# A fused attention and GEGLU kernel on one core: the scale chain split around the scores, one product split, a copy and an eviction exchanged

## The chip, the core and the metric

The kernel runs on one core of one Trainium2 chip. The metric is the device time of one execution in microseconds (us); below, times come from three runs and from one profiled execution. Engines are named as in the profile: PE (TensorE matmul), PEld (its weight loads), DVE (VectorE), ACT (ScalarE), POOL (GpSimd), SP (SyncE, which issues the DMAs).

## What is computed

Two branches of the same x (2048 x 576, float32) are mixed by a gate. Branch a is attention with 32 heads of width 18, in four segments of 512 rows, each with a causal softmax and a compressive memory of the earlier segments. Branch b is a feed-forward layer of width 4608.

```python
x = A_x                                            # 1 x 2048 x 576
g = sigmoid((x * gate_w).sum(-1, keepdims=True))
# a, per head and segment s:
logits = qs @ ks.T * 18**-0.5 + causal_mask
a_dot  = softmax(logits) @ vs
a_mem  = (phi(qs) @ M) / (phi(qs) @ z + 1e-6)      # M, z summed over earlier segments
o      = sigmoid(beta) * a_mem + (1 - sigmoid(beta)) * a_dot
a      = concat(o) @ wo
# b:
b = (gelu(x @ w_gate) * (x @ w_up)) @ w_down
out = g * a + (1 - g) * b
```

## The kernel before

Float32 numbers go through PE as pairs of 16-bit words (a high word and a low word, each product as three matmuls), and some products are formed from sums of blocks, as in Strassen's scheme, so that fewer matmuls are needed. Powers of two scale each pair; they are found from sums of squares of the weights.

After the projections the kernel runs 72 steps, `step(v)` for v = 0 to 71. A step does one 128-column block f = v // 2 of the feed-forward's width for one half p = v % 2 of the rows. Four steps share two blocks f, called a round here: fb = v // 4, i4 = v % 4. Steps 4 to 67 carry one attention head each (k = v - 4; `on(k)` says so) besides the feed-forward work. In step v stand:

- The products of the hidden layer, into three PSUM banks: V, X (the bank "G") and Y (the bank "U"). `product` adds six matmuls, for two 128-row blocks k and three pairs of words each. X gets A11 at the step's start; `dve.tensor_copy(Y, X)` then copies it into Y, and PE goes on adding to both: S2 and S1 to Y, A12 to X. Y's contents are taken to SBUF (`gl` or `hold`) by DVE several times, after which PE adds the next product.
- `down`: the second feed-forward matmul of the round before, in chains of six matmuls of 288 columns into the two banks "dn"; DVE evicts each chain into `acc` (L1283). Three chains (`early`) stand before the scores and five (the rest of `early`, and `late`) behind them.
- `scores`: eight matmuls of the two units 2k and 2k + 1 of a head, into two banks "dn", two "st" and a half each of "pv". A put, `put(a, i)`, is DVE's eviction of one of them with the mask added and the maximum taken (L1189). Unit 2k is put in the same step; of unit 2k + 1 the pieces 1 and 0 are put at the step's end and 3 and 2 (bank "st") in the next step, as `put(2 * k - 1, ...)`.
- `powers` (ACT and POOL): exponentials, a high word on ACT (L1208), a low word by subtraction on POOL (L1209), then a transposing DMA. `values` (PE) and `normalize` (DVE) follow a step later.
- The weights of the next round: `scale_g`, `scale_d` (DVE, L307 and L394), high words on ACT (L341), low words on POOL (L345), sums on POOL.
- Once in a round, in the step i4 = 1, `scales(fb + 1)` computes the powers of two for the next round from a matmul of the sums of squares with ones (L94): a reduction, a multiply with maximum and four bit operations on DVE, all on 2 or 4 columns. `scales_out` makes the scales themselves on POOL (L281 to L289).

Every engine works through its instructions in the order in which the code issues them (`manual_schedule` over PE, ACT, DVE and POOL); only the DMA queue of SP is ordered by the scheduler. So the place of a line in `step` is its place in the engine's queue.

At the end `out_step` does the product with `wo`, in banks of 288 columns that DVE adds into `acc` (L1778), and `store` sends rows out. The last product of all is done in two halves of 144 columns, each with its own eviction and store.

Of the kernel before, what the change touches and what calls it, by code (L numbers as in the profile page):

```python
# [8 lines left out]
F32 = mybir.dt.float32  # L9
BF16 = mybir.dt.bfloat16  # L10
F16 = mybir.dt.float16
I32 = mybir.dt.int32
# [6 lines left out]
P = 128  # L19
# [24 lines left out]
def kernel(ctx: ExitStack, tc: tile.TileContext, xs, wqk, wv, wo, wgu, wd, beta, out):  # L44
# [216 lines left out]

    scl_a = {}

    def scales(fb, o=None):

        o = sums(stat[fb % 2].rearrange("p a b -> p (a b)"), o)
        z = wts.tile([P, 6], F32, name="z", tag="z", bufs=2)
        dve.tensor_reduce(z[:, 4:6], o.rearrange("p (a b) -> p a b", a=2), AX.X, OP.add)
        dve.tensor_scalar(z[:, 0:4], x2, z[:, 4:5], 1e-30, OP.mult, OP.max)  # L269
        v = wts.tile([P, 2, 2], F32, name="v", tag="v", bufs=2)  # L270
        pb = wts.tile([P, 2, 4], F32, name="pb", tag="pb", bufs=3)
        dve.tensor_scalar(v[:, 0].bitcast(I32), z[:, 4:6].bitcast(I32), 1, EXP, OP.logical_shift_right, OP.bitwise_and)
        dve.tensor_scalar(pb[:, 0].bitcast(I32), z[:, 0:4].bitcast(I32), EXP, None, OP.bitwise_and)
        dve.tensor_scalar(v[:, 1].bitcast(I32), v[:, 0].bitcast(I32), EXP, None, OP.bitwise_xor)
        dve.tensor_scalar(pb[:, 1].bitcast(I32), pb[:, 0].bitcast(I32), EXP, None, OP.bitwise_xor)
        scl_a[fb] = v, pb

    def scales_out(fb):
        v, pb = scl_a.pop(fb)
        sc = wts.tile([P, 10], F32, name="sc", tag="sc", bufs=3)  # L280
        pool.tensor_scalar(sc[:, 0:2], v[:, 1], 2.0**-51, None, OP.mult)  # L281
        pool.tensor_scalar(sc[:, 2:6], xis, v[:, 0, 0:1], 2.0**50, OP.mult, OP.mult)
        pool.tensor_scalar(sc[:, 6:10], pb[:, 1], 2.0**14, None, OP.mult)
        pool.tensor_tensor(sc[:, 6:10], sc[:, 6:10], sc[:, 2:6], OP.mult)
        if fb:
            w = wts.tile([P, 4], F32, name="we", tag="we", bufs=2)
            pool.tensor_scalar(w, scl[fb - 1][1][:, 0], v[:, 0, 1:2], 2.0**35, OP.mult, OP.mult)
            ev = wts.tile([P, 16], F32, name="ev", tag="ev", bufs=2)
            pool.tensor_tensor(ev.rearrange("p (c q) -> p c q", c=4),  # L289
                               gate[:, 1].rearrange("p (c q) -> p c q", c=4),  # L290
                               w.unsqueeze(2).to_broadcast([P, 4, 4]), OP.mult)
            evs[fb - 1] = ev
        scl[fb] = (sc, pb)
# [229 lines left out]
    def gl_tile():  # L523
        return mp2.tile([P, L], F32, name="gl", bufs=3)

    def product(o, f, a, x, h, l, start=False):

        w = pair_g[f]
        for k in range(2):
            for i, b in ((0, h), (0, l), (1, h)):  # L530
                pe.matmul(o, w[:, i, (a + k) * P : (a + k + 1) * P], x[:, b + k],  # L531
                          start=start and k == 0 and i == 0 and b == h, stop=k == 1 and i == 1,
                          skip_group_check=True)
# [581 lines left out]
    with tc.tile_pool(name="keep", bufs=2, side="right", reuse_waits="tile") as kp, ExitStack() as tail:  # L1115
# [332 lines left out]
        def step(v):  # L1448
# [33 lines left out]
            if v == 4:  # L1482
                dve.tensor_copy(Y, X)
                nest((1, 0), 2)
                some(0, early[:2])
                nest((1, 0), 3)
                wait = []
                down(0, early[2] // 2, early[2] % 2, wait)
                nest_last(fb, V, p)
                dve.tensor_copy(g1, V)  # L1490
                wait.pop()()
                nest_pairs_x(1, 1)
                some(0, early[3:4])
            elif fb and i4 < 2:
                nest_last(fb, V, p)
                dve.tensor_copy(g1, V)
                dve.tensor_copy(Y, X)
                put(2 * k - 1, 3)
            else:
                put(2 * k - 1, 3)  # L1500
                dve.tensor_copy(Y, X)  # L1501
            if v == 0:
                last_sum(1, 1)
            if v == 1:
# [63 lines left out]
                scales_out(fb + 1)  # L1568
            if both and i4 != 1:
                normalize(k - 2)  # L1570
            product(X, f, A12, x1, 2, 6)
            if v != 3 and not on(k):
                rest(X, f, U4, x1, (0,) if fb else (0, 1))
            if fb > 1 and i4 == 1:
                scales(fb + 1, bank("pv") if on(k) else None)
            some(fb - 1, early[max(one, 2):3])
            if v == 5:
                scales(fb + 1, bank("pv") if on(k) else None)
            product(Y, f, S1, t, 0, 2)
            rest(Y, f, G4, x2_, (0,) if fb else (0, 1))  # L1580
            if v == 3:
                rest(X, f, U4, x1)
            if on(k):
                scores(k, (f, V, G4, x1, 0), (f, X, U4, x1, 0), (f, Y, G4, x2_, 64))
                rest(X, f, U4, x1, (0,))
            elif fb:
                low_rests(f, (V, G4, x1), (Y, G4, x2_))
# [13 lines left out]
                put(2 * k, i)  # L1601
            if low is not None and on(k):
                result_low(low)
            rear = list(early[3 + (v == 4) :])
            if not on(k):
                some(fb - 1, rear)
# [18 lines left out]
            if on(k):  # L1625
                some(fb - 1, rear[:-1])
                nest(at, 0)
                some(fb - 1, rear[-1:])
                nest(at, 1)
                put(2 * k + 1, 1)  # L1630
                puts.pop(2 * k)
                weights_nest(fb, i4, "late")
                powers(2 * k)
                some(fb - 1, late[:1])
                ends.append((f, c, X, g0))
                end_first()
                some(fb - 1, late[1:2])
                nest(at, 2)
                some(fb - 1, late[2:])
                if on(k - 1):  # L1640
                    values(2 * k - 2)
                nest(at, 3)
            else:
                if v != 3:
                    nest(at, 0)
                some(fb - 1, late[:1])
                if v != 3:
                    nest(at, 1)
                weights_nest(fb, i4, "late")
                some(fb - 1, late[1:])  # L1650
                if v != 3:
                    nest(at, 2)
                if on(k - 1):
                    values(2 * k - 2)
                if fb:
                    low_rests(f, (X, U4, x1), (Y, UG, x2_))
                    ends.append((f, c, X, g0))
                    if at or i4 == 1:
                        end_first()
                if v != 3:  # L1660
                    nest(at, 3)
            ends.append((f, e, Y, g1))
# [122 lines left out]
        def out_step(u, p):  # L1785

            x, y = 2 * u, 2 * u + 1
            S = lambda n: lambda i, k: sums_o[u][:, i, 2 * (0, 3, 0, 2, 1)[n] + k]
            A = lambda t, k0: lambda i, k: ot[t][:, 4 * i + k0 + k]
            if p == 7:  # L1790
                V = ob3[u, "V"] = bank("pv" if u % 2 else "V")
                out_product(V, S(3), T3, True)
                out_rest(V, y, R2)
                put_out(V, y, 1)
            if p == 1:
                X, Y = bank("U" if u % 2 else "G"), bank("st", 2)
                ob3[u, "X"], ob3[u, "Y"] = X, Y
                out_product(X, A(x, 0), B11, True)
                dve.tensor_copy(Y[:, :NH], X[:, :NH])
            if p == 4:  # L1800
                V = ob3[u, "V"]
                out_product(V, A(y, 2), T4)
                out_rest(V, y, RD)
                put_out(V, y, 0)
            if p == 2:
                X = ob3[u, "X"]
                out_product(X, A(x, 2), B21)
                out_rest(X, x, R1)
                put_out(X, x, 0)
            if p in (6, 5, 3):  # L1810
                Y = ob3[u, "Y"]
                if (u, p) == (NT - 1, 3):
                    for c in (slice(0, NH // 2), slice(NH // 2, NH)):
                        out_product(Y, S(4), B22, c=c)
                        out_rest(Y, x, R2, c)
                        put_out(Y, x, 1, c)
                        store(x, slice(NH + c.start, NH + c.stop))
                    return
                out_product(Y, S({6: 2, 5: 1, 3: 4}[p]), {6: T2, 5: T1, 3: B22}[p])
                if p == 3:  # L1820
                    out_rest(Y, x, R2)
                put_out(Y, *{6: (y, 0), 5: (y, 1), 3: (x, 1)}[p])
# [6 lines left out]
        with tc.manual_schedule(engines=ORDERED):  # L1829
# [40 lines left out]
            for u in range(NT):  # L1870
# [6 lines left out]
                for i, p in steps:  # L1877
                    out_step(u + i, p)
                    if u == NT - 1:
                        if p == 5:  # L1880
                            store(2 * u + 1, slice(NH, D))
                        if p == 4:
                            store(2 * u + 1, WHOLE)
                if u == NT - 2:
                    store(2 * u + 2, WHOLE)
                if u + 1 < NT:
# [48 lines left out]
```

## Time and profile before

| | before |
|---|---|
| three runs | 1577.87, 1579.21, 1580.11 us; median 1579.21 |
| profiled execution | 1574.72 us, of which the span from first to last instruction 1573.0 |
| granted TensorE clock | 0.999 |
| steps of a usual round (from score to score) | 17.8, 16.9, 19.2 and 19.2 us |
| ACT busy, POOL busy | 77%, 71% of the span |

In a row of the timeline the first number is the start in us from the span's start, the second the duration from the first to the last of the merged instructions; then engine, line and operation, `out<-in`, the shapes, a count, and in brackets how long the engine stood idle before it and what ended that. In a row of the waits stand the waiting engine, tile and line, what it waited for, and then total us, times and the longest. Rows of busy matmuls overlap by some 0.15 us, since their ends are modelled.

### The profile page before, as it was taken

Reading aid. Unit: us, or ns where it says so; the run is one execution under the profiler, and the core shown is the slowest. Engines: PE = TensorE matmul, PEld = TensorE weight load, DVE = VectorE, ACT = ScalarE, POOL = GpSimd, SP = SyncE. Lnnn points to the kernel's source line nnn. Section 1 sums busy time; section 2 is a strip of 40 time slices with the busy share of each in tenths; the row PEclk is TensorE's granted clock in tenths of the full one; section 3 lists DMA queues with packets and bytes.
Section 4 is the critical chain, followed back from the end, with each engine's and each line's share of the span. In section 5 each row is a group of like instructions: output and inputs, shape, how many; then the busy total and the mean of one; then the engine's idle time right before and its main releaser. Section 6 shows DMA issues by size and latency. Waiting matters only on the chain.

```text
span 1573.0 us, 33451 instructions
## 1 busy us (share of the span) xinstructions
PE 1549.2 (98%) x12204; PEld 965.4 (61%) x12204; DVE 1289.8 (82%) x3258; ACT 1213.5 (77%) x2059; POOL 1119.0 (71%) x1217
## 2 busy tenths in 40 slices
PE   9999999999999999999999999999999999999998
PEld 5765655565666656665656565666656566656577
DVE  7878976888888888888898888888888888787675
ACT  7667545888888888988888888888888988887421
POOL 4355566777777868686777777776868687777596
PEclk9999999999999999999999999999999999999999
DMA  6644441464657565566556574756566665555645
GB/s 242 235 151 150 150 130 41 105 138 109 136 118 153 115 136 121 127 133 121 132 113 134 107 153 105 145 114 161 116 139 127 126 138 122 128 104 102 126 86 167
DMA packets 483622, 206.69 MB, mean 131 GB/s; under 512 B 427264, under 2 KB 462464, under 8 KB 482944
## 3 DMA queue, kind: packets, MB, share of 16 engines
q1 hardware_dynamic: 483456, 204.56, 57.1%
q8 instruction: 95, 1.56, 0.4%
q14 instruction: 71, 0.58, 0.1%
HBM read 83.91 MB, written 31.98 MB: 74 GB/s over the span
## 4 chain that ended last, share of the span: by engine, by line
PE 86%; DVE 8%; ACT 2%; POOL 1%; issue 1%; DMA 1%; SPq 0%; POOLq 0%; DVEq 0%; ACTq 0%
PE dn L1273 23%; PE U L531 16%; PE G L531 11%; PE V L531 5%; PE V L1398 5%; PE pv L1226 4%; PE st L412 3%; PE U L1321 2%; PE dn L419 2%; DVE z L269 2%; PE G L412 1%; PE U L412 1%; PE G L1321 1%; PE st L1769 1%; PE U L1325 1%
## 5 line engine op out<-in xcount | busy, mean ns | idle before, releaser
L531 PEld LDWEIGHTS <-pairg 128*128 128x128 f16 x2592 | 247.8, 97 | 259.4 <-issue 10.1
L1273 PE MATMUL dn<-paird,hhr 128*128 128x288 f16 x2115 | 329.9, 286 | 0.1
L1207 ACT ACTIVATE pb<-pb,mb,esc 128x512 f32<-128x512 f32 (+3 forms) x512 | 304.9, 642 | 5.3
L1283 DVE SCALAR_TENSOR_TENSOR acc<-dn,ev,acc 128x288 f32<-128x288 f32 x533 | 267.3, 512 | 48.3 <-PE dn L1273 46.4
L1209 POOL TENSOR_TENSOR pl<-pb,ph 128x896 f16<-128x896 f32 (+1 forms) x128 | 182.0, 1442 | 161.0 <-ACT ph L1208 161.0
L1209 POOL TENSOR_TENSOR pb<-pb,ph 128x896 f16<-128x896 f32 (+1 forms) x128 | 179.5, 1402 | 107.5 <-ACT ph L1208 67.3
L1273 PEld LDWEIGHTS <-hhr 128*128 128x128 f16 x2160 | 210.2, 98 | 74.2 <-issue 1.0
L531 PE MATMUL U<-xt,pairg 128*128 128x512 f16 x864 | 209.9, 379 | 3.5 <-DVE U L1501 3.5
L531 PE MATMUL G<-x,pairg 128*128 128x512 f16 x864 | 209.9, 379 | 0.5 <-DVE gl L1298 0.5
L1273 PE MATMUL dn<-paird,hhd 128*128 128x288 f16 x1275 | 208.6, 286 | 0.0
L1208 ACT ACTIVATE ph<-pb 128x896 f16<-128x896 f32 (+1 forms) x256 | 188.6, 737 | 9.7
L345 POOL TENSOR_TENSOR pairg<-raw,pairg 128x384 f16<-128x384 f32 (+2 forms) x144 | 165.3, 1168 | 17.2 <-ACT pairg L341 17.2
L1273 PEld LDWEIGHTS <-hhd 128*128 128x128 f16 x1296 | 125.6, 98 | 47.4 <-issue 0.5
L1316 ACT ACTIVATE gl<-gl,sc 128x512 f32<-128x512 f32 x110 | 78.6, 717 | 42.2 <-DVE gl L1590 20.9
L1398 PE MATMUL V<-xt,nest 128*128 128x256 f16 x714 | 105.5, 272 | 1.0 <-DVE hold L1422 0.4
L531 PE MATMUL U<-x,pairg 128*128 128x512 f16 x432 | 104.9, 379 | 0.8 <-DVE gl L1590 0.8
L531 PE MATMUL V<-x,pairg 128*128 128x512 f16 x426 | 103.3, 378 | 0.1
L1189 DVE CUSTOM_DVE_ANT_0 pb<-st,mask 128x128 f32<-128x128 f32 (+2 forms) x192 | 96.6, 503 | 0.0
L1189 DVE CUSTOM_DVE_ANT_0 pb<-dn,mask 128x512 f32<-128x512 f32 (+2 forms) x192 | 91.9, 503 | 0.0
L1226 PEld LDWEIGHTS <-pt 128*128 128x128 f16 x2560 | 83.4, 96 | 6.3
L1313 POOL TENSOR_TENSOR hhr<-gl,hhr 128x512 f16<-128x512 f32 x64 | 78.6, 1234 | 11.2 <-ACT hhr L1305 11.2
L412 PEld LDWEIGHTS <-wp 128*128 128x128 f16 x504 | 48.7, 98 | 59.0 <-DVE wp L115 0.9
(367 smaller groups left out, 3244.7 us busy)
## 6 DMA issues: line engine op xcount, KB each, us to landing
raw<-in_wgu_dram SPq DMA_DIRECT2D x36, 640.0 KB
qkt<-qk SPq DMA_DIRECT2D x192, 108.0 KB
rawd<-in_wd_dram SPq DMA_DIRECT2D x36, 288.0 KB
qk<-stage SPq DMA_DIRECT2D x32, 256.0 KB
qk<-stage SPq DMA_DIRECT2D x40, 128.0 KB
vp<-vstage SPq DMA_DIRECT2D x16, 296.0 KB
vt<-vp SPq DMA_DIRECT2D x16, 296.0 KB
orow<-oa SPq DMA_DIRECT2D x16, 288.0 KB
```

Of the source, the lines that this page charges most:

```text
L345: pool.tensor_tensor(spot(f, *p, 1), raw_g[f][:, p[0] : p[1]], spot(f, *p, 0), OP.subtract)
L412: pe.matmul(o, w(k, a), x[:, i], start=n == 0, stop=n == 13, skip_group_check=True)
L531: pe.matmul(o, w[:, i, (a + k) * P : (a + k + 1) * P], x[:, b + k], start=start and k == 0 and i == 0 and b == h, stop=k == 1 and i == 1, ...
L1189: dve.tensor_tensor_reduce(scored(u, qi), out[u, qi], mask[:, L - (qi + 1) * P :], 1.0, -3e38, OP.add, OP.max, mx[u][:, qi : qi + 1])
L1207: act.activation(r, r, AF.Exp, bias=b[:, qi : qi + 1], scale=esc[:, 0, c : c + 1])
L1208: act.activation(h[:, cols], p, AF.Copy)
L1209: pool.tensor_tensor(low[:, cols], p, h[:, cols], OP.subtract)
L1226: pe.matmul(ov, pr[:, 10 * i + COL[qi] // P + kb], v[:, 4 * e + kb, c0 : c0 + VC], start=kb == 0 and i == 0, stop=kb == qi and i == 1)
L1273: pe.matmul(o[:, :NH], hh[:, a, q * P : (q + 1) * P], w[:, b, n * NH : (n + 1) * NH], start=i == 0, stop=i == 5)
L1283: dve.scalar_tensor_tensor(av, o[:, :NH], ev, av, OP.mult, OP.add)
L1313: pool.tensor_tensor(hh[:, 1], t, hh[:, 0], OP.subtract)
L1398: pe.matmul(o, w[:, (7 * c + i) * P : (7 * c + i + 1) * P], x[d], start=start and n == 0, stop=n == 2, skip_group_check=True)
```

## The change

The scale chain of a step i4 = 1 is split. The reduction stays; the multiply with maximum is issued on POOL, behind the score evictions in the text of the step; the bit operations follow there on DVE, with two of them merged into one over six columns. Half of the product A12 for X (its block k = 1) is issued behind the scores in steps that have scores. In steps with i4 of 2 or 3 (and in the first round) the copy of X to Y stands ahead of the put of piece 3 instead of behind it. In the one step behind the last head, the values come two lines later. The last output product is no longer halved.

```diff
--- before.py
+++ after.py
@@ -261,30 +261,37 @@
 
     scl_a = {}
 
-    def scales(fb, o=None):
+    def scales(fb, o=None, later=False):
 
         o = sums(stat[fb % 2].rearrange("p a b -> p (a b)"), o)
         z = wts.tile([P, 6], F32, name="z", tag="z", bufs=2)
         dve.tensor_reduce(z[:, 4:6], o.rearrange("p (a b) -> p a b", a=2), AX.X, OP.add)
-        dve.tensor_scalar(z[:, 0:4], x2, z[:, 4:5], 1e-30, OP.mult, OP.max)
-        v = wts.tile([P, 2, 2], F32, name="v", tag="v", bufs=2)
-        pb = wts.tile([P, 2, 4], F32, name="pb", tag="pb", bufs=3)
-        dve.tensor_scalar(v[:, 0].bitcast(I32), z[:, 4:6].bitcast(I32), 1, EXP, OP.logical_shift_right, OP.bitwise_and)
-        dve.tensor_scalar(pb[:, 0].bitcast(I32), z[:, 0:4].bitcast(I32), EXP, None, OP.bitwise_and)
-        dve.tensor_scalar(v[:, 1].bitcast(I32), v[:, 0].bitcast(I32), EXP, None, OP.bitwise_xor)
+        pb = wts.tile([P, 2, 6], F32, name="pb", tag="pb", bufs=3)
+        scl_a[fb] = z, pb
+        if not later:
+            scales_sum(fb, dve)
+            scales_rest(fb)
+
+    def scales_sum(fb, by):
+        z, pb = scl_a[fb]
+        by.tensor_scalar(z[:, 0:4], x2, z[:, 4:5], 1e-30, OP.mult, OP.max)
+
+    def scales_rest(fb):
+        z, pb = scl_a[fb]
+        dve.tensor_scalar(pb[:, 0, 0:2].bitcast(I32), z[:, 4:6].bitcast(I32), 1, EXP, OP.logical_shift_right, OP.bitwise_and)
+        dve.tensor_scalar(pb[:, 0, 2:6].bitcast(I32), z[:, 0:4].bitcast(I32), EXP, None, OP.bitwise_and)
         dve.tensor_scalar(pb[:, 1].bitcast(I32), pb[:, 0].bitcast(I32), EXP, None, OP.bitwise_xor)
-        scl_a[fb] = v, pb
 
     def scales_out(fb):
-        v, pb = scl_a.pop(fb)
+        _, pb = scl_a.pop(fb)
         sc = wts.tile([P, 10], F32, name="sc", tag="sc", bufs=3)
-        pool.tensor_scalar(sc[:, 0:2], v[:, 1], 2.0**-51, None, OP.mult)
-        pool.tensor_scalar(sc[:, 2:6], xis, v[:, 0, 0:1], 2.0**50, OP.mult, OP.mult)
-        pool.tensor_scalar(sc[:, 6:10], pb[:, 1], 2.0**14, None, OP.mult)
+        pool.tensor_scalar(sc[:, 0:2], pb[:, 1, 0:2], 2.0**-51, None, OP.mult)
+        pool.tensor_scalar(sc[:, 2:6], xis, pb[:, 0, 0:1], 2.0**50, OP.mult, OP.mult)
+        pool.tensor_scalar(sc[:, 6:10], pb[:, 1, 2:6], 2.0**14, None, OP.mult)
         pool.tensor_tensor(sc[:, 6:10], sc[:, 6:10], sc[:, 2:6], OP.mult)
         if fb:
             w = wts.tile([P, 4], F32, name="we", tag="we", bufs=2)
-            pool.tensor_scalar(w, scl[fb - 1][1][:, 0], v[:, 0, 1:2], 2.0**35, OP.mult, OP.mult)
+            pool.tensor_scalar(w, scl[fb - 1][1][:, 0, 2:6], pb[:, 0, 1:2], 2.0**35, OP.mult, OP.mult)
             ev = wts.tile([P, 16], F32, name="ev", tag="ev", bufs=2)
             pool.tensor_tensor(ev.rearrange("p (c q) -> p c q", c=4),
                                gate[:, 1].rearrange("p (c q) -> p c q", c=4),
@@ -523,10 +530,10 @@
     def gl_tile():
         return mp2.tile([P, L], F32, name="gl", bufs=3)
 
-    def product(o, f, a, x, h, l, start=False):
+    def product(o, f, a, x, h, l, start=False, ks=(0, 1)):
 
         w = pair_g[f]
-        for k in range(2):
+        for k in ks:
             for i, b in ((0, h), (0, l), (1, h)):
                 pe.matmul(o, w[:, i, (a + k) * P : (a + k + 1) * P], x[:, b + k],
                           start=start and k == 0 and i == 0 and b == h, stop=k == 1 and i == 1,
@@ -1497,8 +1504,8 @@
                 dve.tensor_copy(Y, X)
                 put(2 * k - 1, 3)
             else:
+                dve.tensor_copy(Y, X)
                 put(2 * k - 1, 3)
-                dve.tensor_copy(Y, X)
             if v == 0:
                 last_sum(1, 1)
             if v == 1:
@@ -1568,20 +1575,21 @@
                 scales_out(fb + 1)
             if both and i4 != 1:
                 normalize(k - 2)
-            product(X, f, A12, x1, 2, 6)
+            product(X, f, A12, x1, 2, 6, ks=(0,) if on(k) else (0, 1))
             if v != 3 and not on(k):
                 rest(X, f, U4, x1, (0,) if fb else (0, 1))
             if fb > 1 and i4 == 1:
-                scales(fb + 1, bank("pv") if on(k) else None)
+                scales(fb + 1, bank("pv") if on(k) else None, on(k))
             some(fb - 1, early[max(one, 2):3])
             if v == 5:
-                scales(fb + 1, bank("pv") if on(k) else None)
+                scales(fb + 1, bank("pv"), True)
             product(Y, f, S1, t, 0, 2)
             rest(Y, f, G4, x2_, (0,) if fb else (0, 1))
             if v == 3:
                 rest(X, f, U4, x1)
             if on(k):
                 scores(k, (f, V, G4, x1, 0), (f, X, U4, x1, 0), (f, Y, G4, x2_, 64))
+                product(X, f, A12, x1, 2, 6, ks=(1,))
                 rest(X, f, U4, x1, (0,))
             elif fb:
                 low_rests(f, (V, G4, x1), (Y, G4, x2_))
@@ -1601,6 +1609,9 @@
                 put(2 * k, i)
             if low is not None and on(k):
                 result_low(low)
+            if on(k) and i4 == 1:
+                scales_sum(fb + 1, pool)
+                scales_rest(fb + 1)
             rear = list(early[3 + (v == 4) :])
             if not on(k):
                 some(fb - 1, rear)
@@ -1650,13 +1661,13 @@
                 some(fb - 1, late[1:])
                 if v != 3:
                     nest(at, 2)
-                if on(k - 1):
-                    values(2 * k - 2)
                 if fb:
                     low_rests(f, (X, U4, x1), (Y, UG, x2_))
                     ends.append((f, c, X, g0))
                     if at or i4 == 1:
                         end_first()
+                if on(k - 1):
+                    values(2 * k - 2)
                 if v != 3:
                     nest(at, 3)
             ends.append((f, e, Y, g1))
@@ -1809,13 +1820,6 @@
                 put_out(X, x, 0)
             if p in (6, 5, 3):
                 Y = ob3[u, "Y"]
-                if (u, p) == (NT - 1, 3):
-                    for c in (slice(0, NH // 2), slice(NH // 2, NH)):
-                        out_product(Y, S(4), B22, c=c)
-                        out_rest(Y, x, R2, c)
-                        put_out(Y, x, 1, c)
-                        store(x, slice(NH + c.start, NH + c.stop))
-                    return
                 out_product(Y, S({6: 2, 5: 1, 3: 4}[p]), {6: T2, 5: T1, 3: B22}[p])
                 if p == 3:
                     out_rest(Y, x, R2)
@@ -1881,6 +1885,8 @@
                             store(2 * u + 1, slice(NH, D))
                         if p == 4:
                             store(2 * u + 1, WHOLE)
+                        if p == 3:
+                            store(2 * u, slice(NH, D))
                 if u == NT - 2:
                     store(2 * u + 2, WHOLE)
                 if u + 1 < NT:
```

On DVE in a step i4 = 1, from the scale chain to the first score eviction, before (x_77 is x2, the squares' sums of x; pb with a number is a score tile, pb alone the scales' bits):

```order
L268 TENSOR_REDUCE z<-pv 128x2
L269 TENSOR_SCALAR z<-x_77,z 128x4
L272 TENSOR_SCALAR v<-z 128x2
L273 TENSOR_SCALAR pb<-z 128x4
L274 TENSOR_SCALAR v<-v 128x2
L275 TENSOR_SCALAR pb<-pb 128x4
L1283 SCALAR_TENSOR_TENSOR acc<-dn,ev,acc 128x288
L1590 TENSOR_TENSOR gl<-U,gl 128x512
L1189 ISA pb_8881,mx<-dn,mask 128x512
```

and in the change, from the reduction on, with the rows between left out:

```order
L268 TENSOR_REDUCE z<-pv 128x2
L1290 SCALAR_TENSOR_TENSOR acc<-dn,ev,acc 128x288
L1598 TENSOR_TENSOR gl<-U,gl 128x512
L1196 ISA pb_8858,mx<-dn,mask 128x512
...
L1196 ISA pb_8859,mx<-pv,mask 128x256
L1196 ISA mx 128x1
L281 TENSOR_SCALAR pb<-z 128x2
L282 TENSOR_SCALAR pb<-z 128x4
L283 TENSOR_SCALAR pb<-pb 128x6
L1290 SCALAR_TENSOR_TENSOR acc<-dn,ev,acc 128x288 x2
```

The eviction of the third early chain follows the reduction at once, and the bit operations stand between the last score eviction and the evictions of the rear chains. The multiply is on POOL now, in the change:

```order
L352 TENSOR_TENSOR pairg<-raw,pairg 128x384
L352 TENSOR_TENSOR pairg<-raw,pairg 128x512
L277 TENSOR_SCALAR z<-x_77,z 128x4
L288 TENSOR_SCALAR sc<-pb 128x2
L289 TENSOR_SCALAR sc<-xis,pb 128x4
```

It stands behind the low words of the weights (L345 before, L352 now) and ahead of `scales_out`, whose first row was the next one before.

On DVE from the end of that step into the step i4 = 2, before:

```order
L394 TENSOR_SCALAR rawd<-rawd,sc 128x576 x2
L1189 ISA pb_8885,mx<-st,mask 128x128
L1189 ISA mx 128x1
L1298 SCALAR_TENSOR_TENSOR gl<-U,sc,gl 128x512
L1189 ISA pb_8884,mx<-st,mask 128x512
L1189 ISA mx 128x1
L1501 COPY U<-G 128x512
L1283 SCALAR_TENSOR_TENSOR acc<-dn,ev,acc 128x288
L1189 ISA pb_8884,mx<-st,mask 128x384
L1189 ISA mx 128x1
L307 TENSOR_SCALAR raw<-raw,sc 128x1280
```

and in the change:

```order
L401 TENSOR_SCALAR rawd<-rawd,sc 128x576 x2
L1196 ISA pb_8862,mx<-st,mask 128x128
L1196 ISA mx 128x1
L1305 SCALAR_TENSOR_TENSOR gl<-U,sc,gl 128x512
L1507 COPY U<-G 128x512
L1196 ISA pb_8861,mx<-st,mask 128x512
L1196 ISA mx 128x1
L1290 SCALAR_TENSOR_TENSOR acc<-dn,ev,acc 128x288
L1196 ISA pb_8861,mx<-st,mask 128x384
L1196 ISA mx 128x1
L314 TENSOR_SCALAR raw<-raw,sc 128x1280
```

The copy has moved ahead of the put of 512 columns; the rest keeps its order.

## The prediction

> **What bounds the kernel now.** I read the page's first and fourth parts, then the waits of PE, then one four-step round of the timeline, engine by engine, then the last five microseconds.
>
> ```profile
> span 1573.0 us, 33451 instructions
> PE 1549.2 (98%) x12204; PEld 965.4 (61%) x12204; DVE 1289.8 (82%) x3258; ACT 1213.5 (77%) x2059; POOL 1119.0 (71%) x1217
> PE 86%; DVE 8%; ACT 2%; POOL 1%; issue 1%; DMA 1%; SPq 0%; POOLq 0%; DVEq 0%; ACTq 0%
> PE dn L1183 <- DVE acc L1283: 10.7, 15, 0.7
> PE U L531 <- DVE U L1501: 3.5, 5, 0.7
> PE U L531 <- DVE gl L1590: 0.8, 1, 0.8
> ```
>
> PE is busy for 1549.2 of 1573.0 us, so a change that removes no matmul can win only what PE waits. The last three rows are the largest such waits in the body (total us, times, longest us): 15.0 us together, all on DVE. The place of the 10.7 us is the step with v % 4 = 1, once in every round of four steps. One such step on DVE, POOL, ACT and PE (start, duration, instruction, idle before it in brackets):
>
> ```profile
> 649.30 0.17 DVE L268 TENSOR_REDUCE z<-pv 128x2 f32<-128x10 f32 x1 [0.57 <-PE pv L94]
> 649.50 1.93 DVE L269 TENSOR_SCALAR z<-x,z 128x4 f32<-128x4 f32 x1
> 651.34 0.16 DVE L272 TENSOR_SCALAR v<-z 128x2 int32<-128x2 int32 x1
> 651.54 0.89 DVE L274 TENSOR_SCALAR v<-v 128x2 int32<-128x2 int32 x1
> 652.41 0.51 DVE L1283 SCALAR_TENSOR_TENSOR acc<-dn,ev,acc 128x288 f32<-128x288 f32 x1
> 652.84 0.68 DVE L1590 TENSOR_TENSOR gl<-U,gl 128x512 f32<-128x512 f32 x1
> 655.68 0.08 DVE L1189 DVE_READ_ACCUMULATOR2_ANT mx<- 128x1 f32 x1
> 656.23 0.52 DVE L1283 SCALAR_TENSOR_TENSOR acc<-dn,ev,acc 128x288 f32<-128x288 f32 x1 [0.48 <-PE dn L1273]
> 649.51 2.89 POOL L1209 TENSOR_TENSOR pb<-pb,ph 128x896 f16<-128x896 f32 x2 [1.71 <-ACT ph L1208]
> 653.55 0.72 ACT L1316 ACTIVATE gl<-gl,sc 128x512 f32<-128x512 f32 x1 [0.45 <-DVE gl L1590]
> 654.76 0.72 ACT L1316 ACTIVATE gl<-gl,sc 128x512 f32<-128x512 f32 x1 [0.49 <-DVE gl L1598]
> 652.37 2.03 POOL L345 TENSOR_TENSOR pairg<-raw,pairg 128x384 f16<-128x384 f32 x2
> 654.37 0.22 POOL L281 TENSOR_SCALAR sc<-v 128x2 f32<-128x2 f32 x1
> 649.83 1.46 PE L531 MATMUL U<-xt,pairg 128*128 128x512 f16 x6
> 651.88 0.38 PE L1183 MATMUL dn<-qkt 54*128 54x512 f16 x1
> 652.97 0.32 PE L1183 MATMUL dn<-qkt 54*128 54x384 f16 x1 [0.71 <-DVE acc L1283]
> 653.57 1.46 PE L531 MATMUL U<-x,pairg 128*128 128x512 f16 x6
> 655.29 3.91 PE L1273 MATMUL dn<-paird,hhr 128*128 128x288 f16 x30
> ```
>
> The reader is to see why four-element work costs DVE 3.1 us. L269 starts at 649.50 and POOL's two subtractions (L1209) at 649.51; L269 runs 1.93 us, and L274 (0.89 us) ends at 652.43, where POOL's pair ends (649.51 + 2.89 = 652.40). L272, of the same kind, takes 0.16. So two of the steps stand while a POOL instruction runs. Behind them on DVE waits the eviction at 652.41; the second score bank (652.97) waits for that eviction. From first to second dn score is 1.09 us here.
>
> **The change, part by part.**
>
> *The scale chain.* In a step v % 4 = 1 the sum's reduction stays where it is. L269 goes to POOL, behind the two L345 rows; three of the four bit steps go behind the score evictions, and one is gone by merging. So after 649.47 DVE takes the eviction at once, about 2.5 us ahead of 652.41, and the second dn score finds its bank free. The price is the difference between 1.09 us and the spacing of the same two scores in a step without the chain:
>
> ```profile
> 669.70 0.38 PE L1183 MATMUL dn<-qkt 54*128 54x512 f16 x1
> 669.91 0.38 PE L1183 MATMUL dn<-qkt 54*128 54x384 f16 x2
> ```
>
> That is 0.21 us, so 0.88 us a step, 15 times: 13.2 us. The sixteenth (v = 5) shows as the 0.8 us on L1590. Together -14.0.
>
> What is late next? DVE reaches the moved bit steps when the score evictions are done. They took from 652.84 (L1590) to 655.76; L1590 can now start when its sum is ready, which I estimate at the first dn score less the 0.65 us below, 651.2, so DVE arrives at 654.1. POOL is free at 652.37 + 2.03 = 654.40. The moved multiply is not in the trace on POOL; its nearest row is L281, 0.22 us. So DVE's second bit step can go at about 654.7 and the third is done near 655.1 (0.16 us each). Behind it is queued the first eviction of the rear chains, which comes 0.94 us after PE's chains start (656.23 against 655.29); those start 0.88 earlier, so it is due at 655.35. The wait for POOL of 0.6 us is thus covered by DVE's own idle time, with 0.2 us to spare; without that cover each further us of lateness would reach PE. POOL's six result instructions start 0.7 us later and end near 657; its next work is the row at 660.12 below. I take 0 for this, bounds 0 and 0.4 us a step.
>
> *Half of X behind the scores.* Three of the six L531 matmuls on G go behind the scores. From 653.57 to 655.29 stand six such and two more of that width, 1.72 us for eight, so three are 0.65 us; the scores come that much earlier and no PE time is added; the G weights cost the same in either place. It gives DVE 0.65 us more between the scores and PE's next need of U, and takes 0.65 us from every eviction that must be done before the scores.
>
> *The copy ahead of an eviction* (v % 4 = 2 and 3). Rows of the step that follows, first a usual round, then one of those with a wait:
>
> ```profile
> 659.68 0.94 DVE L394 TENSOR_SCALAR rawd<-rawd,sc 128x576 f32<-128x576 f32 x2
> 661.40 0.68 DVE L1189 CUSTOM_DVE_ANT_0 pb<-st,mask 128x512 f32<-128x512 f32 x1
> 662.33 0.70 DVE L1501 COPY U<-G 128x512 f32<-128x512 f32 x1 [0.24 <-PE G L531]
> 663.98 1.07 DVE L307 TENSOR_SCALAR raw<-raw,sc 128x1280 f32<-128x1280 f32 x1
> 668.32 0.51 DVE L1283 SCALAR_TENSOR_TENSOR acc<-dn,ev,acc 128x288 f32<-128x288 f32 x1
> 660.12 3.12 POOL L1209 TENSOR_TENSOR pl<-pb,ph 128x896 f16<-128x896 f32 x2 [3.93 <-ACT ph L1208]
> 663.21 2.85 POOL L1313 TENSOR_TENSOR hhr<-gl,hhr 128x512 f16<-128x512 f32 x2
> 585.53 2.65 DVE L394 TENSOR_SCALAR rawd<-rawd,sc 128x576 f32<-128x576 f32 x2
> 589.58 0.69 DVE L1501 COPY U<-G 128x512 f32<-128x512 f32 x1
> 590.32 1.46 PE L531 MATMUL U<-xt,pairg 128*128 128x512 f16 x6 [0.72 <-DVE U L1501]
> ```
>
> In the usual round the put (661.40 to 662.08) fits into the time before G is ready. Behind the copy, its 0.68 us pushes all that follows, since from 662.33 to the eviction that ends at 668.83 DVE has almost no idle time. That eviction frees the bank of the score at 669.91: a slack of 1.08 us. It loses 0.65 (scores earlier) and 0.68 (put later): 1.08 - 0.65 - 0.68 = -0.25. And L307 now asks at 664.66, when the second of POOL's two L1313 has begun (663.21 plus half of 2.85); I estimate that as 0.3 us more. So a new wait of 0.2 to 0.6 us arises in the step v % 4 = 2.
>
> In the blocked round the two L394 took 2.65 us instead of 0.94 and PE waited 0.72 for the copy. There the swap takes the put's 0.68 us out of PE's way, and the later bank wait comes in its stead, so it ends in the same range. I take 0.4 us for either, 16 times: +6.4; bounds 0 (if DVE makes it up) and 1.3 (L394 blocked and L307 blocked after it). The 3.5 us of waits for L1501 go: -3.5. In steps v % 4 = 3 the same shift stays inside the idle time before L1551; no charge.
>
> *The tail.*
>
> ```profile
> 1567.71 0.54 PE L1769 MATMUL st<-wo,x 128*128 128x144 f16 x6
> 1568.83 0.54 PE L1769 MATMUL st<-wo,x 128*128 128x144 f16 x6 [0.46 <-DVE acc L1778]
> 1569.53 0.37 DVE L1778 SCALAR_TENSOR_TENSOR acc<-st,gate,acc 128x144 f32<-128x144 f32 x1 [0.75 <-PE st L1774]
> ```
>
> The last sum in two column halves ends at 1569.90. A half takes 0.70 us from its first matmul to its eviction (1568.83 to 1569.53), so the whole at most 1.40, to 1569.1 without the 0.46 wait, and one eviction of 0.52 (the 128x288 form at 656.23) ends near 1569.6. The last store is 144 KB instead of 72, cost not shown, so between -0.4 and +0.4; I take -0.3.
>
> The move of the values in the step v = 68, the merged bit step and the swapped SP issues have idle queues around them: 0.
>
> Sum: -14.0 - 3.5 + 6.4 - 0.3 = -11.4 us on the profiled execution's 1574.72, so 1563.3. That execution is 4.5 us under the median of the runs shown, 1579.21. The blocked rounds are decided by hundredths of a us: L394 starts 0.44 us ahead of POOL's pair in both rounds (659.68 and 660.12; 585.53 and the row below).
>
> ```profile
> 585.97 2.97 POOL L1209 TENSOR_TENSOR pl<-pb,ph 128x896 f16<-128x896 f32 x2 [3.94 <-ACT ph L1208]
> ```
>
> So I think part of the 4.5 us is further blocked rounds, which the change makes no dearer than the others. From the median the sum gives 1567.8, from the profile 1563.3; I forecast 1565.
>
> **The rivals.**
>
> *Full gain.* DVE, 2.5 us less loaded in the round, makes up the put, and no wait arises at v % 4 = 2: -17.8, 1557 by the profile, 1561 by the median. Against it: the copy waits for G at 662.33 however early DVE is, so the time won before it cannot be carried past it.
>
> *Slower: L394 blocked in every round.* ACT and POOL also move: ACT's two waits of this step, 0.45 and 0.49 on L1590 and L1598, end with the scale chain, so ACT goes 0.94 us earlier and PE 0.88. Then POOL's pair asks 0.06 us sooner against L394 than at 660.12, and takes its turn between the two L394 each time, 1.71 us longer (2.65 - 0.94). If L307 then also meets a POOL instruction (one L1313 is half of 2.85 us), the bank for the score is late by 1.3 us or more, and 16 x 1.3 = 20.8 eats the 17.8: 1578 by the profile, 1582 by the median. It decides from 17.8 / 16 = 1.1 us a round. For it: the block happened in this very trace. Against: in the blocked round the eviction still kept up with PE, so both must be met together. The Trainium skill, "SBUF — State Buffer", Who interferes with whom, has the rule behind it: VectorE and GpSimd share one port pair as an exclusive lock, and whoever starts first keeps it for the whole instruction. The rows at 649.50 and 585.53 agree; by it the change only moves which instruction meets the lock.
>
> *POOL late.* If the moved multiply comes 0.6 us later than I think, DVE stands 0.4 us past its cover and PE waits at the rear chains: 16 x 0.4 = 6.4 back, 1570 to 1574. POOL's place at 654.40 hangs on ACT alone, and it came at the same distance in the rounds I read; hence little.
>
> **How the numbers follow.** The forecast case (net 8 to 16 us) 0.63, its own range 1559 to 1571. Full gain 0.14. POOL late 0.10. Slower rival, whole or in part, 0.13, of which about half ends within or above the time before. What a measurement can tell from no change is 0.2%, 3.2 us. Faster 0.86, same 0.07, slower 0.07. The range of 8 in 10 runs from the lower edge of the full gain, 1557, to the upper edge of POOL late, 1574.
>
> **What would show it.** Right: the row PE dn L1183 <- DVE acc is gone from steps v % 4 = 1 and a smaller one stands at v % 4 = 2; the multiply on POOL takes about 0.25 us; the bit steps take 0.16 us each; U <- L1501 is gone. Wrong: PE waits at the rear chains for evictions behind the bit steps, or L394 at 2.6 us in all rounds with PE waits of over 1 us behind it.

## The result and the profile after

The changed kernel takes 1564.41 us (median of 4 runs, 1564.22 to 1565.15) against 1579.24 us before (4 runs, 1577.87 to 1580.11): a ratio of 0.9908, 95% interval 0.9891 to 0.9925. It is 14.8 us faster by the medians and 10.5 us faster by the two profiled executions (1564.22 against 1574.72). The forecast was 1565.

The page's first part, and the waits of PE (engine, tile and line, what it waited for; total us, times, longest). Lines of the changed kernel are 6 to 11 higher than before: L1183 is now L1190, L1501 L1507, L394 L401.

```profile
span 1562.1 us, 33442 instructions
PE 1550.3 (99%) x12196; PEld 967.7 (62%) x12196; DVE 1257.6 (81%) x3222; ACT 1210.0 (77%) x2059; POOL 1123.9 (72%) x1233
PE U L538 <- DVE U L1507: 4.3, 16, 0.8
```

PE's busy time is nearly what it was (1549.2 before); what has gone is waiting. The 10.7 us at the second dn score have no row any more. The waits for the copy, 3.5 us in 5 rounds before, are now 4.3 us in 16 rounds.

The timeline of one step v % 4 = 1, DVE, then POOL, then PE:

```profile
645.82 0.17 DVE L268 TENSOR_REDUCE z<-pv 128x2 f32<-128x10 f32 x1
646.55 0.52 DVE L1290 SCALAR_TENSOR_TENSOR acc<-dn,ev,acc 128x288 f32<-128x288 f32 x1 [0.56 <-PE dn L1280]
651.22 0.37 DVE L281 TENSOR_SCALAR pb<-z 128x2 int32<-128x2 int32 x1
652.00 0.17 DVE L282 TENSOR_SCALAR pb<-z 128x4 int32<-128x4 int32 x1 [0.41 <-POOL z L277]
652.21 0.17 DVE L283 TENSOR_SCALAR pb<-pb 128x6 int32<-128x6 int32 x1
652.46 0.52 DVE L1290 SCALAR_TENSOR_TENSOR acc<-dn,ev,acc 128x288 f32<-128x288 f32 x1
646.68 2.89 POOL L1216 TENSOR_TENSOR pb<-pb,ph 128x896 f16<-128x896 f32 x2 [1.98 <-ACT ph L1215]
651.66 0.31 POOL L277 TENSOR_SCALAR z<-x,z 128x4 f32<-128x4 f32 x1
648.40 0.38 PE L1190 MATMUL dn<-qkt 54*128 54x512 f16 x1
648.62 0.38 PE L1190 MATMUL dn<-qkt 54*128 54x384 f16 x2
651.53 3.91 PE L1280 MATMUL dn<-paird,hhr 128*128 128x288 f16 x30
```

The dn scores are 0.22 us apart, as in any other step. DVE waits 0.41 us for POOL's multiply, and L281 takes 0.37 us instead of the 0.16 of its kind; it ends with POOL's second L352 (at 651.57). The last bit step ends at 652.38, and the first rear eviction starts at 652.46, which is 0.94 after the start of PE's chains, as in the kernel before. So PE still sets the time of this eviction: the wait is hidden, with about 0.1 us to spare.

The same round in the step v % 4 = 2:

```profile
655.91 2.58 DVE L401 TENSOR_SCALAR rawd<-rawd,sc 128x576 f32<-128x576 f32 x2
659.46 0.70 DVE L1507 COPY U<-G 128x512 f32<-128x512 f32 x1
661.58 0.88 DVE L314 TENSOR_SCALAR raw<-raw,sc 128x1280 f32<-128x1280 f32 x1
656.25 3.00 POOL L1216 TENSOR_TENSOR pl<-pb,ph 128x896 f16<-128x896 f32 x2 [1.98 <-ACT ph L1215]
660.21 1.46 PE L538 MATMUL U<-xt,pairg 128*128 128x512 f16 x6 [0.23 <-DVE U L1507]
665.88 0.38 PE L1190 MATMUL dn<-qkt 54*128 54x512 f16 x1
```

POOL's pair now starts 0.34 us behind the first L401 (0.44 before), gets ahead of the second, and the two take 2.58 us; below such a round is called blocked. So it is in 15 of the 16 rounds; in the first one the pair comes ahead of both. PE waits 0.23 us for the copy. From dn score to dn score this step takes 665.88 - 648.40 = 17.48 us; before it was 669.70 - 651.88 = 17.82 in a usual round, with the 0.88 us between the two dn scores in it.

### The profile page after: what moved, and what is told of

Read it like the earlier page. It is cut to its first block, busy times and chain, and to the rows that moved or that the text cites. A ratio compares the mean times of both kernels' runs of the same rounds, so it can differ in the third digit from the quotient of the medians.

```text
span 1562.1 us, 33442 instructions
## 1 busy us (share of the span) xinstructions
PE 1550.3 (99%) x12196; PEld 967.7 (62%) x12196; DVE 1257.6 (81%) x3222; ACT 1210.0 (77%) x2059; POOL 1123.9 (72%) x1233
## 5 line engine op out<-in xcount | busy, mean ns | idle before, releaser
L538 PEld LDWEIGHTS <-pairg 128*128 128x128 f16 x2592 | 242.5, 97 | 266.0 <-issue 23.8
L1216 POOL TENSOR_TENSOR pb<-pb,ph 128x896 f16<-128x896 f32 (+1 forms) x128 | 187.7, 1467 | 118.6 <-ACT ph L1215 94.7
L538 PE MATMUL G<-x,pairg 128*128 128x512 f16 x864 | 221.0, 380 | 0.0
L352 POOL TENSOR_TENSOR pairg<-raw,pairg 128x384 f16<-128x384 f32 (+2 forms) x144 | 157.6, 1115 | 17.2 <-ACT pairg L348 17.2
L1323 ACT ACTIVATE gl<-gl,sc 128x512 f32<-128x512 f32 x110 | 75.2, 712 | 26.0 <-DVE gl L1598 13.7
L348 ACT ACTIVATE pairg<-raw 128x384 f16<-128x384 f32 (+2 forms) x144 | 77.8, 587 | 8.9 <-DVE raw L314 6.5
```

The costliest lines, as they stand in the source:

```text
L348: act.activation(spot(f, *p, 0), raw_g[f][:, p[0] : p[1]], AF.Copy)
L352: pool.tensor_tensor(spot(f, *p, 1), raw_g[f][:, p[0] : p[1]], spot(f, *p, 0), OP.subtract)
L1216: pool.tensor_tensor(low[:, cols], p, h[:, cols], OP.subtract)
L1323: act.activation(t, o, AF.Gelu_apprx_tanh, scale=scl[f // 2][0][:, 2 + c : 3 + c])
```

## Experiments

Times are medians; a ratio is to runs of the kernel before on the same chip. The kernel before was not equally fast each time: 1574.25 us (1570.30 to 1578.40) beside k1 to k4, 1578.44 (1576.62 to 1582.24) beside k5, k6, k7 and k9, 1570.23 (1569.74 to 1570.87) beside k8 and k10; the first and the last of these are from the same chip. The variants spread by 0.4 to 1.5 us each (k9 by 2.1), so times of the variants are compared with each other; k7 shows why the kernel before is different. A round is the sum of four steps from dn score to dn score, 73.05 us before when nothing is blocked and 72.73 in the change.

**k1: the chain alone.** The kernel before with `scales` split as in the change; product, copy and tail as before.

> The kernel before with only the scale chain split (reduction in place, multiply on POOL and three bit steps on DVE behind the score evictions). Theory A (PE loses what it waits for DVE, and DVE loses what it waits for POOL): the wait of 0.7 us at the second dn score goes in all rounds (-14.0 us), but ACT and POOL come earlier, so L394 is blocked in all 16 rounds instead of 4, and the copy, still behind the put, costs PE 0.88 us in 12 more rounds (+10.6): 1571 us, L394 pairs at 2.6 us, U <- L1501 16 times at 0.7 us. Rival B (the chain is the whole gain, the other parts do nothing): 1564 to 1565 us and U <- L1501 as seldom as before.

1572.16 us, ratio 0.9985 (0.9976 to 0.9994).

```profile
PE U L538 <- DVE U L1508: 11.5, 16, 1.2
657.70 2.62 DVE L401 TENSOR_SCALAR rawd<-rawd,sc 128x576 f32<-128x576 f32 x2
```

As theory A has it: the wait at the dn score went, L401 was blocked in every round, and PE waited 0.7 us for the copy 16 times. The chain's move alone gives all of its gain back: a usual round is 73.19 us, against 73.05 before when nothing is blocked. Of the 0.88 us it loses 0.73 up to the next score (17.73 against the 17.00 of k6 below), and another 0.22 in the step after v % 4 = 3 (19.38 against 19.16; see k4).

**k2: the chain undone.** The changed kernel without the chain's move.

```diff
-                scales(fb + 1, bank("pv") if on(k) else None, on(k))
+                scales(fb + 1, bank("pv") if on(k) else None)
...
-            if on(k) and i4 == 1:
-                scales_sum(fb + 1, pool)
-                scales_rest(fb + 1)
```

> The changed kernel with the whole scale chain back on DVE ahead of the scores; half product, copy and tail stay as changed. Theory A: what stalled the chain was POOL's pair, which began 0.01 us after L269 asked. With half of X behind the scores the reduction ends 0.65 us earlier, at about 0.7 us ahead of POOL's pair, so the multiply takes 0.23 us and all steps are through before the pair starts: 1563 to 1566 us, no wait at the second dn score. Rival B (moving the chain is what saves): L269 stays at 1.9 us, and PE waits 0.9 + 0.65 us a round: 1585 to 1590 us.

1563.74 us (1563.46 to 1564.09), ratio 0.9931 (0.9917 to 0.9946); a round is 72.72 us. The chain's place on DVE, and POOL's pair:

```profile
646.56 0.17 DVE L268 TENSOR_REDUCE z<-pv 128x2 f32<-128x10 f32 x1
646.76 0.23 DVE L277 TENSOR_SCALAR z<-x,z 128x4 f32<-128x4 f32 x1
647.23 0.17 DVE L283 TENSOR_SCALAR pb<-pb 128x6 int32<-128x6 int32 x1
647.31 0.51 DVE L1290 SCALAR_TENSOR_TENSOR acc<-dn,ev,acc 128x288 f32<-128x288 f32 x1
647.42 2.89 POOL L1216 TENSOR_TENSOR pb<-pb,ph 128x896 f16<-128x896 f32 x2 [1.98 <-ACT ph L1215]
L277 DVE TENSOR_SCALAR z<-x,z x19: 229/229/1906, 161.7 to 1447.2; 128x4 f32<-128x4 f32 x19
```

The last row has the shortest, median and longest duration in ns. The same multiply that took 1.93 us takes 0.23, since it now asks 0.66 us ahead of POOL's pair instead of together with it; only in the first round the two still meet (1.91 us). So the chain need not be moved: with half of X behind the scores PE reaches the sum's matmul 0.65 us earlier, and that alone takes the chain out of the pair's way. Counted from the start of PE's rear chains in the step before, the reduction starts after 14.14 us in the kernel before and after 13.49 in k2, and POOL's pair after 14.35 in both.

**k3: the copy undone.** The changed kernel with `put(2 * k - 1, 3)` ahead of the copy again.

> The changed kernel with the copy behind the put again. Theory A: L401 stays blocked in every round, so the copy comes 0.61 to 0.68 us later in the steps v % 4 = 2; PE waits 0.9 instead of 0.23 us for it, and the wait of 0.2 us at the scores is taken up by that: 16 x 0.45 to 0.65 = 7 to 10 more, 1571 to 1575 us. Rival C (the copy ahead of the put only pushes the put, as in the prediction's slack of -0.25 us): 1560 to 1564 us.

1567.95 us (1567.81 to 1568.22), ratio 0.9958 (0.9944 to 0.9973).

```profile
PE U L538 <- DVE U L1508: 10.9, 16, 1.2
```

So 3.5 us worse than the change. The sign is theory A's, the size is half of it: the waits for the copy grew by 6.6 us (10.9 less 4.3), but a step v % 4 = 2 only from 17.48 to 17.69 us, since PE lost part of this at the scores already.

**k4: the half product undone.** The changed kernel with the whole of A12 ahead of the scores.

> The changed kernel with the whole product A12 ahead of the scores again. Theory A: the bit steps wait for POOL's multiply and not for the evictions ahead of them, so they end at the same distance from the rear chains; only the wait of about 0.2 us for the pv bank at the scores of v % 4 = 2 goes: 1561 to 1563 us. Rival D (the earlier scores are what gives DVE the time for the chain): the bit steps come 0.65 us later, PE waits at the rear chains, 1568 to 1575 us.

1564.25 us (1563.64 to 1564.68), ratio 0.9934 (0.9919 to 0.9948): no change either, where 1561 to 1563 was expected. The step v % 4 = 2 did become 0.17 us shorter (17.31), but the step after v % 4 = 3 took 19.31 instead of 19.16. There the low words of the attention result (L1263, which reads two SBUF tiles on DVE) met POOL: 1.18 us instead of 0.82. First k4, then the change:

```profile
686.00 1.18 DVE L1263 SCALAR_TENSOR_TENSOR ob<-ob,wsc,oh 128x576 f16<-128x576 f32 x1
683.68 2.89 POOL L1216 TENSOR_TENSOR pb<-pb,ph 128x896 f16<-128x896 f32 x2 [0.88 <-ACT ph L1215]
685.59 0.82 DVE L1263 SCALAR_TENSOR_TENSOR ob<-ob,wsc,oh 128x576 f16<-128x576 f32 x1
683.69 3.49 POOL L1216 TENSOR_TENSOR pb<-pb,ph 128x896 f16<-128x896 f32 x2 [0.88 <-ACT ph L1215]
```

In k4 the second of POOL's two starts 0.35 us ahead of L1263, and L1263 is late; in the change it starts 0.07 behind, and POOL's pair is late, which costs PE nothing.

**k9: both undone.** The changed kernel with k2's and k4's edits together.

> The changed kernel with both the scale chain and the whole product A12 put back; only the copy, the tail and the values two lines later stay as changed. Theory A (the chain's move and the half product each take the chain out of POOL's way, and either is enough): L277 takes 1.9 us again and PE waits 0.7 us at the second dn score in all rounds, so 1564 + 16 x 0.88 less what the later PE hides, 1572 to 1578 us. Rival G (the gain is the copy and the tail): 1564 us.

1574.59 us (1573.56 to 1575.68), ratio 0.9975 (0.9965 to 0.9985).

```profile
PE dn L1190 <- DVE acc L1290: 9.6, 15, 0.6
PE U L538 <- DVE U L1507: 3.6, 12, 0.3
L277 DVE TENSOR_SCALAR z<-x,z x19: 229/1919/1927, 160.7 to 1457.1; 128x4 f32<-128x4 f32 x19
```

The median of L277 is back at 1.92 us and so is the wait. Each of the two parts is enough, and without both the gain at the dn scores is gone. L401 was blocked in 12 of the 16 rounds. What is left, 3.9 us against the kernel before beside it, was not taken apart: it holds the tail, the values, the merged bit step and the copy, with which a blocked round costs 0.34 us (73.58 against 73.24) instead of the 1.09 of k7.

**k8: the multiply on VectorE.** The changed kernel with `scales_sum(fb + 1, dve)` at the late place.

> The changed kernel with the moved multiply on DVE at its late place instead of on POOL. Theory A: the multiply and the three bit steps now ask while POOL's two L352 run and wait for their end as they waited for POOL's multiply; the end comes out at the same time, so 1563 to 1566 us. Rival H (POOL is what makes the place work): DVE is late at the rear chains, 1568 us or more.

1562.81 us (1562.38 to 1563.83); a round is 72.72 us, as in the change; of the 1.0 us between the two spans 0.9 lie in the first round. POOL's part in the change has no effect that shows: DVE's own multiply took 0.37 us in the median, waiting for the end of POOL's L352 instead of for POOL's multiply.

**k7: the spread of the kernel before.** The second L394 of a round goes to the step v % 4 = 3, where DVE has idle time.

```diff
                 scale_g(n0 + 2)
+            if i4 == 3 and 0 < fb < NB - 1:
+                scale_d(n0 + 1)
...
-                for f in (2 * fb, 2 * fb + 1):
-                    scale_d(f)
+                scale_d(2 * fb)
```

> The kernel before with the second L394 multiply moved in the same way, nothing else. Theory A (the spread of the kernel before, 1570 to 1580 us, is the number of its rounds in which POOL's pair gets ahead of the second L394, each 1.07 us): no round can be blocked, so 1570 to 1571 us with a spread under 1 us. Rival F (the spread comes from elsewhere, as from the DMA): the median and the spread stay, 1574 us.

1569.42 us (1568.66 to 1569.61), ratio 0.9943 (0.9930 to 0.9955), beside runs of the kernel before of 1576.62 to 1582.24.

```profile
PE dn L1183 <- DVE acc L1283: 10.7, 15, 0.7
679.00 2.04 DVE L394 TENSOR_SCALAR rawd<-rawd,sc 128x576 f32<-128x576 f32 x1
```

The wait at the dn scores is untouched, the row for L1501 is gone, and the runs lie within 1 us. The moved multiply meets POOL in its new place as well (2.04 us), but no wait of PE comes of it there. So the spread is the number of blocked rounds, at 1.09 us each (74.14 against 73.05 a round). The profiled execution of the kernel before had five, the first round and four others, and its span is 5.1 us longer than k7's. Of the 1.09 us, 0.86 fall into the step with the wait for the copy (18.68 against 17.82) and 0.2 into the step after v % 4 = 3: in the same four rounds the low words of the result (L1256, the L1263 of the change) met POOL too, and took 1.23 us instead of 0.82. A row of the kernel before:

```profile
616.14 1.23 DVE L1256 SCALAR_TENSOR_TENSOR ob<-ob,wsc,oh 128x576 f16<-128x576 f32 x1
```

The lowest run of the kernel before was 1569.74, as with none. So the size of the gain hangs on the runs that it is measured against: 14.8 us here, of which by these figures some 10 us (an estimate, from 1579.24 less the 1569.42 of k7) are blocked rounds of the kernel before, and about 5 us against its lowest run.

**k5 and k6: towards a better version.** k5 is the change with k7's edit; k6 is k5 with the copy behind the put again.

> The changed kernel with the second of the two L401 multiplies (the round's second w_down block) moved from the end of the step v % 4 = 1 to the start of the step v % 4 = 3. Theory A: POOL's pair then finds nothing of DVE in its way and blocks nothing; DVE reaches the copy before G is ready, U <- L1507 goes to 0, and of the 0.54 us lost between the scores of v % 4 = 1 and 2 there remain 0.2 to 0.45 us, the put behind the copy: 1557 to 1562 us. Rival E (the 0.54 us is the put behind the copy, and the blocked multiply only fills time in which DVE would wait for G): 1564 us.

> The same with the copy behind the put again. Theory A: unblocked, the put fits into the wait for G, and nothing is late at the scores: the whole 0.54 us go in 16 rounds, 1555 to 1557 us, and no row PE <- DVE of more than 0.3 us a round is left. Rival E: as k3, 1568 us.

k5: 1560.89 us (1560.48 to 1561.20), ratio 0.9889 (0.9876 to 0.9903). k6: 1556.83 us (1556.47 to 1556.98), ratio 0.9864 (0.9849 to 0.9879). In k6:

```profile
653.25 0.51 DVE L401 TENSOR_SCALAR rawd<-rawd,sc 128x576 f32<-128x576 f32 x1
654.55 0.68 DVE L1196 CUSTOM_DVE_ANT_0 pb<-st,mask 128x512 f32<-128x512 f32 x1
655.91 0.70 DVE L1509 COPY U<-G 128x512 f32<-128x512 f32 x1 [0.67 <-PE G L538]
657.55 1.75 DVE L314 TENSOR_SCALAR raw<-raw,sc 128x1280 f32<-128x1280 f32 x1
653.60 2.79 POOL L1216 TENSOR_TENSOR pl<-pb,ph 128x896 f16<-128x896 f32 x2 [2.00 <-ACT ph L1215]
645.74 0.38 PE L1190 MATMUL dn<-qkt 54*128 54x512 f16 x1
662.74 0.38 PE L1190 MATMUL dn<-qkt 54*128 54x512 f16 x1
```

The remaining L401 starts 0.34 us ahead of POOL's pair and takes its 0.51 us, the put fits into the wait for G, and the step takes 17.00 us instead of 17.48, though L314 is held up to 1.75 us. In k5 the put behind the copy still cost: its step after v % 4 = 2 took 17.25 instead of 16.88, with a wait at the scores (L1250, 12 times). So the copy ahead of the put helps while DVE is late, and harms once it is not.

**k10.** k6 with the chain back ahead of the scores as in k2.

> k6 (second L401 multiply later, copy behind the put) with the whole scale chain back on DVE ahead of the scores; the half product stays behind them. Theory A: the chain runs before POOL's pair as in k2 and costs nothing, so 1555.5 to 1557.5 us, the same as k6: of the change's parts the half product alone does the work. Rival B: over 1560 us.

1556.07 us (1555.55 to 1556.57), ratio 0.9909 (0.9894 to 0.9924) to a kernel before that ran at 1570.23 beside it; a round is 72.23 us, as in k6 (72.24).

```profile
L277 DVE TENSOR_SCALAR z<-x,z x19: 229/229/1916, 161.4 to 1439.2; 128x4 f32<-128x4 f32 x19
```

The best version has the half product and the later weight, and neither the moved chain nor the exchanged copy.

## Why the prediction was right, point by point

- **The number.** 1564.41 against 1565, but the terms missed by up to 1.6 us each and their errors cancelled: by the figures below the chain was worth -13.0 (-14.0 forecast), the blocked rounds of the profiled execution -5.1 (-3.5), the new loss +7.7 (+6.4), the tail -0.9 (-0.3), together -11.3 where -11.4 was forecast (-10.5 measured). That the errors cancel is luck, and so is the place of 1565 between 1563.3 and 1567.8. The chances do not quite add up either: the three faster cases make 0.87, and with the half of the slower rival that ends below the time before, faster would be about 0.93 instead of 0.86.
- **The bound.** Right. PE's busy time lay between 1546.4 and 1551.4 us in all profiles; the span moved from 1554.7 to 1573.0 with PE's waits.
- **The scale chain, -14.0.** The wait went in all rounds, near its size: k6's round of 72.24 against 73.05 is 0.81 us a round, 13.0 us in 16, where the term had 0.88. But the credit was wrong. The term was put down to the chain's move, and the half product was said to give DVE 0.65 us and to take 0.65 us from evictions. That step failed: the half product also brings the reduction 0.65 us forward, ahead of POOL's pair, which the rows at 649.50 and 649.51 allowed to be worked out. k2 and k4 show that either part does it, k9 that one must.
- **POOL's multiply, cost 0.** Right. 0.31 us instead of the 0.22 of its nearest row, and 0.37 for the first bit step instead of 0.16; of the cover of 0.2 us about 0.1 was left. k8 shows that the engine does not matter there.
- **The copy, -3.5, and the new wait, +6.4.** The net of +2.9 came out near what was measured (7.7 less 5.1), with another share. The -3.5 counted only PE's waits for L1501; the five blocked rounds cost 5.1 (k7). Steps v % 4 = 2 lost 17.48 - 17.00 = 0.48 us a round, 7.7 us in all; 0.4 was forecast. That they lost it by L401 blocked in every round was in the slower rival, as was its cause (ACT and POOL earlier than PE). That rival needed L314 to be blocked too; L314 took 0.88 us there, and its bound of 1.1 us a round was not reached. The waits for the copy did not go, they became short. The wait that was forecast at the scores, 0.2 to 0.6 us, is the small part: from PE's last product to the first score are 0.42 us (665.23 to 665.65), 0.33 in k6, so about 0.1 of the 0.48 lies there and the rest at the copy.
- **The tail, -0.3.** Mis-sized: from the last product's first matmul to the end it took 1573.0 - 1567.71 = 5.29 us before, and the rows below give 1562.1 - 1557.69 = 4.41, so -0.88, outside the bounds. Of this, 0.49 lie before the end of the last eviction, for which 0.3 was forecast, and 0.39 behind it: the larger store did not take longer, from there to the end it is 2.71 us after, 3.10 before. Why it took less is not shown.

```profile
1557.69 0.90 PE L1780 MATMUL st<-wo,x 128*128 128x288 f16 x6
1558.87 0.52 DVE L1789 SCALAR_TENSOR_TENSOR acc<-st,gate,acc 128x288 f32<-128x288 f32 x1 [0.46 <-PE st L1785]
```

- **Profile and median.** -11.4 was forecast on the profiled execution, -10.5 was measured. The guess that the other 4.5 us were further blocked rounds is supported by k7, whose runs lie within 1 us and whose profile has no blocked round.
- **The signs.** The row PE dn <- DVE went and the multiply took about what was said; the row U <- L1501 did not go (4.3 us in 16 rounds), and one bit step took 0.37 us. Of the signs of being wrong, L401 at 2.6 us in all rounds came, but PE waited 0.23 us behind it and not over 1.
- **The port rule.** The rule named from the Trainium skill, "SBUF — State Buffer", Who interferes with whom, fits where the starts lie well apart: one multiply took 0.23 us when it started 0.66 us ahead of POOL's pair (k2). The rows at 649.50 and 585.53, which the prediction says agree, show that one engine held the other up, but not that the first to start went first: L269 and the second L394 start 0.01 and 0.02 us ahead of POOL by the profile, and both waited. At such distances the recorded starts do not decide it. The rule was used for the slower rival alone; applied to the reduction's new place it would have given the right credit.

What stays open is why POOL's pair slips between two L394 in some executions and rounds and not in others, on the same chip too; that was not tried.

## What to carry to other kernels

Where two engines hold each other up, a gain is a matter of who asks first: before moving work, work out for each moved matmul what small instructions it brings forward or back against the other engine's long ones. Parts of one change can be substitutes, so undo them one by one and together. An engine that a change sets free brings its own next work forward, and that can meet a second collision; here clearing both was worth 8 us more than the change.

## What was not expected of the hardware

- Two DVE instructions back to back leave room for POOL. With 0.44 us between the first L394's start and POOL's, POOL went ahead of the second in 4 of 15 rounds before and in 11 of 15 in k9; with 0.41 (k1, k4) or 0.34 us (the change) in all 15. By k7 this makes the spread of the kernel before, 1570 to 1582 us.
- DVE's subtraction with two SBUF inputs met POOL too: L1263 took 0.82 or 1.18 us.
- A four-element multiply took 0.31 us on POOL and 0.23 us on DVE; on DVE together with POOL's subtraction it took 1.92.
